# A gated convolution and MLP mixer on one core: weight loads on another queue, some row sums on another engine, fused small arithmetic and a new written-out order

## The chip, the core and the metric

The kernel runs on one NeuronCore of a Trainium2 chip. Five engines work side by side, each with its own instruction list: TensorE (PE in the profile, with PEld for its weight loads), VectorE (DVE), ScalarE (ACT), GpSimd (POOL) and SyncE (SP). SyncE does no arithmetic; it issues DMA transfers. ScalarE and GpSimd can issue transfers too. The engines meet only through semaphores. The metric is the device time of one execution in microseconds (us), as the median of several runs.

## The reference, cut to what matters

The input is a sequence of S = 2048 rows with D = 640 features, all in bfloat16. Two branches are mixed by a gate for each row.

```python
x = A_q
g = sigmoid((x * gate_w).sum(-1, keepdims=True))
# branch a: shift convolution (4 taps) of k, times v, then a long convolution with ssm_k by FFT
kv = k_shift * v
y  = irfft(rfft(kv, 2S) * rfft(ssm_k, 2S))[:S] + kv * ssm_D
a  = x * y
# branch b: norm, w1, gelu, shift of four feature groups by +-1 and +-2 rows, w2; norm, w3, gelu, w4
h  = gelu(layernorm(x) @ w1)
x1 = x + shifted(h) @ w2
b  = x1 + gelu(layernorm(x1) @ w3) @ w4
return g * a + (1 - g) * b
```

layernorm subtracts the row's mean and divides by the root of its variance plus 1e-5.

## The kernel before, in words

Rows are worked in 16 tiles of 128 (t = 0 to 15), grouped in four chunks of 512 (sc = 0 to 3). Features are worked in 5 groups of 128 (c = 0 to 4) in the convolution branch. All data lives in one SBUF tensor called `arena`, and all PSUM in one called `PSall` with 8 banks. So the profile names every operand `arena` or `PSall`, and helper functions give many operations the same line: L657 is every tensor_tensor of VectorE, L662 every plain tensor_scalar, L667 every activation, L689 nearly every matmul, L234 and L237 every DMA.

The stages are these. `x_load` brings the rows of x; `ln1` takes each tile's mean and variance, has GpSimd raise the variance to the power -1/2 (L862), normalises the tile on VectorE and transposes it (tiles 0 to 7 on TensorE at L919, the rest by DMA); `mm1` multiplies by w1 and ScalarE applies the gelu; `mm2` multiplies the shifted result by w2 and adds x; `ln2`, `mm3`, `mm4` do the second half of the MLP. Beside that, for each feature group, `h_load` and `h_fold` prepare the filter, `kv` forms the four-tap convolution times v, `h_chunk` and `x_fwd` are the Fourier transforms as matmuls, `unit` multiplies the spectra on VectorE, and `final` transforms back and mixes.

Nothing is scheduled on the fly. The program first records every operation, with a number, and then emits them in the order of a hand-supplied table of numbers, `SEQUENCE`; each engine runs its own operations in that order. `PLACES` says which PSUM bank each accumulation takes, and `ON` is a string of switches that moves single operations (a scaling, a copy, an addition) between VectorE and ScalarE, or between VectorE and a DMA. An engine that waits holds back everything behind it in its list, SyncE included: a transfer that waits for its data delays the transfers behind it.

What the steps below touch. The mean and variance of the first norm come from VectorE's bn_stats (two halves of a tile, L858) and bn_aggr (L859) for all 16 tiles, since `LNS` is 16; the branch for tiles from `LNS` on is there but empty. w1 is loaded in two halves of 400 KB each and w2 in one part of 640 KB and four of 40 KB; all seven are issued by ScalarE. A VectorE copy at L732 gathers a part of both halves of w1 into `w1x`. `hx` copies (L943) move 32-row pieces of the gelu's output to their shifted places. `mmg` is the gate's dot product on TensorE, whose four results a chunk VectorE copies out of PSUM.

```python
PET, LNS, LNA = 8, 16, 4
        P.dma("act", w1[:, :, 320 * h:320 * (h + 1)], ...
    P.dma("act", w2[:, 0:4, :], ...
```

Of the kernel before, what the change touches and what calls it, by code (L numbers as in the profile page):

```python
# [8 lines left out]
ACTF = mybir.ActivationFunctionType  # L9
# [434 lines left out]
def bass_gated_mix__ssm_conv_h3__mixer_s_mlp__prompt_kernel(  # L444
# [6 lines left out]
    P = Prog(nc)  # L451
# [27 lines left out]
    def ps(n, cls):  # L479
# [3 lines left out]
    SEQUENCE = [7, 2, 1, 0, 5, 3, 6, 46, 8, 9, 4, 10, 11, 12, 13, 14, 15, 16, 17, 18, 19, 20, 21, 22, 45, 48, 52,  # L483
# [67 lines left out]
    ON = ("0000000011111111010100000010000000000100001011110000000000000010000000001101001000010100100111110010"  # L551
          "00100100001000100000000000000000000010000000000")

    HW = S + 4
    oXF = alloc(20480)
# [606 lines left out]
```

## Time and profile before

| What | Value |
|---|---|
| Median of 3 runs | 226.66 us |
| The runs | 1255.35, 226.16, 226.66 us |
| The profiled execution's own time | 224.96 us |
| Its span in the trace | 223.2 us |
| Granted TensorE clock | 0.995 of full |
| TensorE busy | 210.7 us (94%) |
| VectorE busy | 213.0 us (95%) |
| ScalarE busy | 192.6 us (86%) |
| GpSimd busy | 53.6 us (24%) |

The span is the time from the first instruction to the last in the trace; the execution's own time holds 1.8 us around it. The run of 1255.35 us is far from the other two and the median does not depend on its size. Durations in the text come from the profiled execution. The busy time of an engine is the union of its instructions' times; neighbouring instructions overlap a little, so the mean duration of one is more than the time by which it moves its engine on.

### The profile page before, as it was taken

What the parts mean: (1) busy time and instruction counts of PE and PEld (TensorE: products, weight loads), DVE (VectorE), ACT (ScalarE), POOL (GpSimd) and SP (SyncE); (2) the same over time, 40 slices, a digit from 0 to 9 for tenths busy, and PEclk for the clock granted to TensorE, in tenths of its full rate; (3) what the DMA queues carried; (4) which work ended last, traced back from release to release, by engine and by line L of the source; (5) the groups of instructions that cost most, each with busy time, mean ns of one, the idle gap of its engine ahead of it and who ended that gap; (6) DMA issues with size and microseconds to landing.
All of it is one profiled execution on the core that took longest, in us unless ns stands there. A gap on an engine that the chain in (4) does not pass through costs nothing.

```text
span 223.2 us, 3880 instructions
## 1 busy us (share of the span) xinstructions
PE 210.7 (94%) x1418; PEld 126.8 (57%) x1418; DVE 213.0 (95%) x434; ACT 192.6 (86%) x304; POOL 53.6 (24%) x57
## 2 busy tenths in 40 slices
PE   5599999999999999999999999999999999999960
PEld 2297875544566444675445665445666545777640
DVE  5999999998999998999999999999997999999994
ACT  2278999999989999998999999999999797466891
POOL 1221201240000320000132102106216662475340
PEclk9999999999999999999999999999999999999997
DMA  5996799997799994999556879699399999988788
GB/s 148 348 255 218 107 243 230 179 267 161 152 232 332 295 310 97 204 187 202 110 109 118 175 151 226 116 188 200 72 187 172 261 164 245 175 102 96 82 118 167
DMA packets 80803, 41.30 MB, mean 185 GB/s; under 512 B 59210, under 2 KB 77327, under 8 KB 80783
## 3 DMA queue, kind: packets, MB, share of 16 engines
q1 hardware_dynamic: 72080, 30.42, 59.0%
q0 software_dynamic: 6496, 8.92, 26.8%
q10 hardware_dynamic: 2206, 1.71, 2.7%
q8 instruction: 11, 0.18, 0.4%
q14 instruction: 10, 0.07, 0.1%
HBM read 14.88 MB, written 5.77 MB: 93 GB/s over the span
## 4 chain that ended last, share of the span: by engine, by line
DVE 69%; DMA 11%; ACT 8%; PE 7%; issue 2%; ACTq 1%; POOLq 0%
DVE arena L657 59%; ACT arena L667 8%; DMA arena<-arena 7%; PE PSall L689 7%; DMA arena<-in_B_w_dram 4%; DVE arena L662 4%; DVE arena L858 3%; DVE arena L943 2%; DVE arena L978 1%; ACTq L237 1%; DVE arena L859 1%; ACT L715 0%; DVE arena L732 0%; ACT arena L715 0%; POOLq L389 0%
## 5 line engine op out<-in xcount | busy, mean ns | idle before, releaser
L689 PE MATMUL PSall<-arena 128*128 128x512 bf16 (+5 forms) x1357 | 203.0, 309 | 3.6 <-DVE arena L657 1.9
L657 DVE TENSOR_TENSOR arena<-arena 128x1024 bf16<-128x1024 bf16 (+14 forms) x279 | 174.7, 688 | 2.6 <-DMA arena<-arena 1.0
L689 PEld LDWEIGHTS PSall<-arena 128*128 128x128 bf16 x1357 | 122.6, 98 | 83.1 <-ACT arena L667 3.2
L667 ACT ACTIVATE arena<-PSall 128x512 bf16<-128x512 f32 (+8 forms) x157 | 96.4, 673 | 14.8 <-PE PSall L919 8.5
L667 ACT ACTIVATE arena<-arena 128x640 bf16<-128x640 bf16 (+5 forms) x89 | 82.9, 959 | 3.5 <-DVE arena L657 3.4
L862 POOL TENSOR_TENSOR arena<-arena 128x2 f32<-128x2 f32 (+2 forms) x15 | 17.4, 1161 | 70.2 <-DVE arena L662 36.2
L237 POOL DMA_DIRECT2D arena<-arena x14 | 12.4, 886 | 77.6 <-DVE arena L657 71.5
L237 POOL DMA_DIRECT2D out_dram<-arena x24 | 24.6, 1299 | 16.1 <-ACT arena L667 8.3
L667 ACT ACTIVATE arena<-PSall,arena 128x640 bf16<-128x640 f32 (+2 forms) x32 | 20.3, 657 | 6.9 <-PE PSall L689 6.8
L858 DVE BATCH_NORM_STATS2 arena<-arena 128x6 f32<-128x320 bf16 x32 | 14.4, 480 | 1.7 <-DMA arena<-in_A_q_dram 1.6
L662 DVE TENSOR_SCALAR arena<-arena 128x640 bf16<-128x640 bf16 (+8 forms) x51 | 13.8, 289 | 0.1
L978 DVE SCALAR_TENSOR_TENSOR arena<-PSall,arena 128x640 bf16<-128x640 f32 x12 | 9.7, 814 | 0.5 <-PE PSall L689 0.5
L712 PE MATMUL PSall<-arena 128*128 128x512 bf16 x15 | 5.3, 521 | 2.3 <-DVE arena L709 2.3
L919 PE MATMUL PSall<-arena 128*128 128x128 bf16 x40 | 3.5, 219 | 2.0 <-DVE arena L662 2.0
L712 PEld LDWEIGHTS PSall<-arena 128*128 128x128 bf16 x15 | 1.8, 129 | 5.0 <-issue 2.4
L943 DVE TENSOR_SCALAR arena<-arena 32x256 bf16<-32x256 bf16 (+1 forms) x18 | 4.1, 229 | 0.3
L919 PEld LDWEIGHTS PSall<-arena 128*128 128x128 bf16 x40 | 2.4, 97 | 2.9 <-DVE arena L662 2.2
L859 DVE BATCH_NORM_AGGREGATE arena<-arena 128x2 f32<-128x12 f32 x16 | 2.8, 193 | 0.1
L667 ACT ACTIVATE PSall<-PSall 128x640 f32<-128x640 f32 x4 | 2.8, 698 | 0.1
L667 ACT ACTIVATION_READ_ACCUMULATOR arena<-arena 128x1 f32 x12 | 2.4, 198 | 0.0
L715 ACT ACT_TABLE_LOAD x1 | 1.3, 1283 | 1.2 <-PEq L1147 1.2
L662 DVE TENSOR_SCALAR arena<-PSall 128x4 f32<-128x4 f32 x4 | 0.6, 156 | 0.3 <-PE PSall L689 0.3
(22 smaller groups left out, 5.5 us busy)
## 6 DMA issues: line engine op xcount, KB each, us to landing
arena<-arena POOLq DMA_DIRECT2D x8, 512.0 KB, 5.8
arena<-in_A_ssm_k_dram SPq DMA_DIRECT2D x5, 512.0 KB, 4.5
arena<-in_A_q_dram SPq DMA_DIRECT2D x6, 320.0 KB, 6.1
arena<-in_B_w_dram SPq DMA_DIRECT2D x1, 1920.0 KB, 10.1
out_dram<-arena SPq DMA_DIRECT2D x16, 96.0 KB, 3.4
arena<-arena POOLq DMA_DIRECT2D x6, 256.0 KB, 3.4
out_dram<-arena POOLq DMA_DIRECT2D x16, 96.0 KB, 5.0
arena<-in_A_q_dram SPq DMA_DIRECT2D x8, 192.0 KB, 4.7
```

The costliest lines, as they stand in the source:

```text
L237: fn = lambda e: e.dma_start(out, in_, **kw)
L657: P.op(eng, lambda e: e.tensor_tensor(o, real(a), real(b), op), [a, b], [o], dve_ns(o, [a, b], 2) if eng == "dve" else 500)
L662: P.op(eng, lambda e: e.tensor_scalar(o, real(a), s1, s2, op0=op0, **({} if op1 is None else {"op1": op1})), [a] + aps, [o], dve_ns(o, [a] ...
L667: P.op("act", lambda e: e.activation(real(o), real(a), f, bias=bias, scale=scale, **({"accum_out": accum} if accum is not None else {})), ...
L689: fns.append(lambda e, l=l, r=r, i=i: e.matmul(real(o), l, r, start=(i == 0), stop=(i == last)))
L712: P.op("pe", lambda e: e.matmul(real(pw), warm[:, 0:128], warm[:, 128:640], start=True, stop=True), [warm], [pw], 427.0 if i < 14 else 216.0)
L858: P.op("dve", lambda e, o=o, i=i: e.bn_stats(o, i), [i], [o], 400)
L859: P.op("dve", lambda e: e.bn_aggr(bna[:, t, :], bns[k]), [bns[k]], [bna[:, t, :]], 120)
L862: P.op("pool", lambda g: g.tensor_tensor(o, a, e, ALU.pow), [a, e], [o], dur)
L919: P.op("pe", [lambda e, c=c, pb=pb, xn=xn: e.transpose(real(pb)[:, 128 * c:128 * (c + 1)], xn[:, 128 * c:128 * (c + 1)], ident) for c in r ...
L943: P.op("dve", lambda e, o=hT[q, 4, c0:c0 + n], i=hx[q, :]: e.tensor_scalar(o, i, 1.0, None, op0=ALU.mult), [hx[q, :]], [hT[q, 4, c0:c0 + n ...
L978: P.op("dve", lambda e: e.scalar_tensor_tensor(x, real(pr), 1.0, x, op0=ALU.mult, op1=ALU.add, accum_out=st[1, 0][:, t:t + 1]), [pr, x], [ ...
```

## The change

Six things change together.

1. The loads of w1 and w2 are issued by SyncE instead of ScalarE.
2. `LNS` goes from 16 to 12: for tiles 12 to 15 the row sum and the sum of squares of the first norm come from two ScalarE passes with an accumulated output, in place of bn_stats and bn_aggr on VectorE.
3. The small arithmetic on the norms' statistics and on the gate uses scalar_tensor_tensor, which does two operations in one instruction; the second norm's normalisation becomes x * rstd + off on VectorE too.
4. ScalarE instead of VectorE copies the gate's dot products out of PSUM.
5. `ON` sets other switches. Counted in the built programs: two of the 128x2048 tap scalings, one copy of 1x1024, one normalisation and three 128x256 scalings go from ScalarE to VectorE, three copies of 1x512 go the other way; four more `hx` copies of 32x512 are on VectorE instead of SyncE; three more additions of 128x1024 are on VectorE and one of 128x2048 fewer (the others are accumulating DMAs of GpSimd).
6. `SEQUENCE` and `PLACES` are new throughout.

The core of the diff; of the two tables only the first line is shown.

```diff
-    SEQUENCE = [7, 2, 1, 0, 5, 3, 6, 46, 8, 9, 4, 10, 11, 12, 13, 14, 15, 16, 17, 18, 19, 20, 21, 22, 45, 48, 52,
...
+    SEQUENCE = [2, 1, 5, 4, 0, 26, 3, 8, 9, 10, 11, 12, 13, 14, 15, 16, 25, 45, 50, 49, 17, 18, 48, 28, 68, 51, 27,
...
-    st = {(l, f): small(NT) for l, f in [(0, 3), (0, 5)] + [(1, f) for f in range(6)]}
+    st = {(l, f): small(NT) for l, f in [(0, 3), (0, 5)] + [(1, f) for f in (0, 1, 3, 4, 5)]}
...
-    st.update({(0, 0): bna[:, :, 1], (0, 1): gst[3], (0, 4): gst[5]})
+    st.update({(0, 1): gst[3], (0, 4): gst[5]})
...
-        P.dma("act", w1[:, :, 320 * h:320 * (h + 1)], B_w1[:, 320 * h:320 * (h + 1)].rearrange("(c p) f -> p c f", p=128),
+        P.dma(sp, w1[:, :, 320 * h:320 * (h + 1)], B_w1[:, 320 * h:320 * (h + 1)].rearrange("(c p) f -> p c f", p=128),
               bias=(9.5e8, 8.9e8)[h], early=True).lat += 400.0
...
-    P.dma("act", w2[:, 0:4, :], bass.AP(B_w2.tensor, B_w2.offset, [[D, 128], [160 * D, 4], [1, D]]), bias=5e8, early=True)
+    P.dma(sp, w2[:, 0:4, :], bass.AP(B_w2.tensor, B_w2.offset, [[D, 128], [160 * D, 4], [1, D]]), bias=5e8, early=True)
     for g in range(4):
-        P.dma("act", w2[32 * g:32 * (g + 1), 4, :], B_w2[160 * g + 128:160 * g + 160, :], bias=4e8, early=True)
+        P.dma(sp, w2[32 * g:32 * (g + 1), 4, :], B_w2[160 * g + 128:160 * g + 160, :], bias=4e8, early=True)
...
+    def stt(o, a, x, b, op0, op1):
+        aps = [x] if not isinstance(x, float) else []
+        P.op("dve", lambda e: e.scalar_tensor_tensor(o, a, x, b, op0=op0, op1=op1), [a, b] + aps, [o], n_of(o) / 0.96 + 65)
...
             if a >= LNS:
-                var_of(0, a, b)
-                ts(bna[:, a:b, 0], st[0, 0][:, a:b], 1.0 / D, None, ALU.mult)
+                tt(st[0, 4][:, a:b], mean, mean, ALU.mult)
+                stt(st[0, 3][:, a:b], st[0, 1][:, a:b], 1e-5, st[0, 4][:, a:b], ALU.add, ALU.subtract)
...
-    def var_of(l, a, b):
-        s = {f: st[l, f][:, a:b] for f in (0, 1, 3, 4)}
-        tt(s[4], s[0], s[0], ALU.mult)
-        ts(s[4], s[4], 1.0 / D ** 2, 1e-5, ALU.mult, ALU.subtract)
-        tt(s[3], s[1], s[4], ALU.subtract)
-
     def ln_math(l, a, b):
-        var_of(l, a, b)
-        pool_pow(st[l, 5][:, a:b], st[l, 3][:, a:b], neghalf[:, a:b])
-        ts(st[l, 2][:, a:b], st[l, 0][:, a:b], -1.0 / D, None, ALU.mult)
-        tt(st[l, 4][:, a:b], st[l, 2][:, a:b], st[l, 5][:, a:b], ALU.mult)
+        s = {f: st[l, f][:, a:b] for f in (0, 1, 3, 4, 5)}
+        stt(s[4], s[0], 1.0 / D ** 2, s[0], ALU.mult, ALU.mult)
+        stt(s[3], s[1], 1e-5, s[4], ALU.add, ALU.subtract)
+        pool_pow(s[5], s[3], neghalf[:, a:b])
+        stt(s[4], s[0], -1.0 / D, s[5], ALU.mult, ALU.mult)
...
-    PET, LNS, LNA = 8, 16, 4
+    PET, LNS, LNA = 8, 12, 4
...
-            act(xn1[t // 2 % 2][:, t % 2], X[:, t, :], ACTF.Copy, accum=st[0, 0][:, t:t + 1])
+            act(xn1[t // 2 % 2][:, t % 2], X[:, t, :], ACTF.Copy, scale=1.0 / D, accum=bna[:, t, 0:1])
...
-        ts(gst[0][:, 4 * sc:4 * sc + 4], pg, 1.0, None, ALU.mult)
+        scale(gst[0][:, 4 * sc:4 * sc + 4], pg, 1.0, False)
...
-        ts(gst[2], bna[:, :, 0], gsum[:, 0:1], None, ALU.mult)
-        tt(gst[1], gst[1], gst[2], ALU.add)
+        stt(gst[1], bna[:, :, 0], gsum[:, 0:1], gst[1], ALU.mult, ALU.add)
...
-                ts(xn, x, mean, rstd, ALU.add, ALU.mult)
+                ts(xn, x, rstd, off, ALU.mult, ALU.add)
```

SyncE's list from its start, before the change: `in_A_q_dram` is x, `in_A_ssm_k_dram` the filter, `in_A_k_dram` is k.

```order
L237 DMA arena<-in_A_q_dram 128x640 x3
L237 DMA arena<-in_A_q_dram 128x2x640
L237 DMA arena<-in_A_q_dram 128x640
L237 DMA arena<-in_A_q_dram 128x2x640 x3
L237 DMA arena<-in_A_ssm_k_dram 128x2048
L234 DMA_TRANSPOSE arena<-in_A_k_dram 128x2048
L237 DMA arena<-in_A_q_dram 128x2x640 x2
L234 DMA_TRANSPOSE arena<-arena 128x16x128
```

The same list after the change, from its second row on (four single tiles of x stand ahead of it); 128x5x320 is a half of w1, 32x640 and 128x4x640 are parts of w2, and the transpose of 128x16x128 is that of the folded filter of group 0.

```order
L237 DMA arena<-in_A_q_dram 128x2x640
L237 DMA arena<-in_B_w_dram 128x5x320 x2
L237 DMA arena<-in_A_q_dram 128x2x640
L237 DMA arena<-in_B_w_dram 32x640
L237 DMA arena<-in_A_ssm_k_dram 128x2048
L237 DMA arena<-in_A_q_dram 128x2x640
L237 DMA arena<-in_B_w_dram 32x640 x2
L237 DMA arena<-in_A_q_dram 128x2x640
L234 DMA_TRANSPOSE arena<-in_A_k_dram 128x2048
L237 DMA arena<-in_B_w_dram 32x640
L234 DMA_TRANSPOSE arena<-arena 128x16x128
L237 DMA arena<-in_B_w_dram 128x4x640
```

w1 now stands behind the first six tiles of x, and the large part of w2 stands behind the transposes of k and of the folded filter.

VectorE's list just ahead of the copy into `w1x`, before the change: the copy is the row at L732.

```order
L858 BN_STATS arena<-arena 128x6 x2
L859 BN_AGGR arena<-arena 128x2 x3
L662 TENSOR_SCALAR arena<-arena 128x1
L662 TENSOR_SCALAR arena<-arena 128x640
L858 BN_STATS arena<-arena 128x6 x3
L732 TENSOR_SCALAR arena<-arena 128x640
L662 TENSOR_SCALAR arena<-arena 128x2
L858 BN_STATS arena<-arena 128x6
```

The same place after the change, where the copy is the row at L731.

```order
L857 BN_STATS arena<-arena 128x6
L661 TENSOR_SCALAR arena<-arena 128x1
L857 BN_STATS arena<-arena 128x6 x2
L858 BN_AGGR arena<-arena 128x2
L731 TENSOR_SCALAR arena<-arena 128x640
L858 BN_AGGR arena<-arena 128x2
L661 TENSOR_SCALAR arena<-arena 128x640
L661 TENSOR_SCALAR arena<-arena 128x2
```

The copy has moved forward: 12 bn_stats of VectorE stand ahead of it now, and 15 stood there before.

ScalarE's list after the change, at the place where `mm2` of the tiles 0 to 3 is taken from PSUM: a plain 128x640 from `arena` to `arena` is a pass of the first norm's sums of tiles 12 to 15.

```order
L666 ACTIVATE arena<-PSall 128x4
L666 ACTIVATE arena<-arena 128x640
L666 ACTIVATE PSall,arena<-PSall 128x2x320
L666 ACTIVATE arena<-arena 128x640 x2
L666 ACTIVATE arena<-PSall 128x640 x2
L666 ACTIVATE PSall,arena<-PSall 128x2x320
L666 ACTIVATE arena<-arena 128x640 x2
L666 ACTIVATE PSall,arena<-PSall 128x2x320
L666 ACTIVATE arena<-arena 128x640 x2
```

Seven of the eight new passes stand between these evictions of PSUM; the eighth follows a little later.

More of the change, by code (lines that the diff above doesn't have):

```diff
@@ L481, in ps @@
         return v if n == 1 else v.rearrange("p (b n) -> p b n", b=2)
-    SEQUENCE = [7, 2, 1, 0, 5, 3, 6, 46, 8, 9, 4, 10, 11, 12, 13, 14, 15, 16, 17, 18, 19, 20, 21, 22, 45, 48, 52,
[60 rows of a table removed]
-    PLACES = [5, 3, 4, 3, 7, 2, 6, 4, 0, 5, 3, 5, 1, 0, 7, 5, 2, 2, 0, 6, 5, 2, 7, 0, 1, 0, 4, 3, 2, 6, 5, 2, 1, 0,
[6 rows of a table removed]
-    ON = ("0000000011111111010100000010000000000100001011110000000000000010000000001101001000010100100111110010"
-          "00100100001000100000000000000000000010000000000")
+    SEQUENCE = [2, 1, 5, 4, 0, 26, 3, 8, 9, 10, 11, 12, 13, 14, 15, 16, 25, 45, 50, 49, 17, 18, 48, 28, 68, 51, 27,
[59 rows of a table added]
+    PLACES = [7, 0, 4, 2, 5, 7, 5, 7, 4, 2, 0, 5, 4, 0, 1, 6, 6, 2, 5, 4, 1, 7, 4, 1, 4, 1, 3, 6, 2, 2, 1, 1, 0, 6,
[6 rows of a table added]
+    ON = ("0000000011111111111111110101110110010100010000101111000000100000011000000000110000000001010010001001"
+          "001000100100001000000000000000000000000000101001001")
     HW = S + 4
@@ L865, in bn_math @@
         for a, b in ((t0, t1),) if t0 >= 4 else ((t, t + 1) for t in range(t0, t1)):
+            mean, var = bna[:, a:b, 0], bna[:, a:b, 1]
             if a >= LNS:
-                var_of(0, a, b)
-                ts(bna[:, a:b, 0], st[0, 0][:, a:b], 1.0 / D, None, ALU.mult)
+                tt(st[0, 4][:, a:b], mean, mean, ALU.mult)
+                stt(st[0, 3][:, a:b], st[0, 1][:, a:b], 1e-5, st[0, 4][:, a:b], ALU.add, ALU.subtract)
             else:
-                ts(st[0, 3][:, a:b], bna[:, a:b, 1], 1e-5, None, ALU.add)
+                ts(st[0, 3][:, a:b], var, 1e-5, None, ALU.add)
             pool_pow(st[0, 5][:, a:b], st[0, 3][:, a:b], neghalf[:, a:b], 750)
-    def var_of(l, a, b):
-        s = {f: st[l, f][:, a:b] for f in (0, 1, 3, 4)}
-        tt(s[4], s[0], s[0], ALU.mult)
-        ts(s[4], s[4], 1.0 / D ** 2, 1e-5, ALU.mult, ALU.subtract)
-        tt(s[3], s[1], s[4], ALU.subtract)
-    def ln_math(l, a, b):
-        var_of(l, a, b)
-        pool_pow(st[l, 5][:, a:b], st[l, 3][:, a:b], neghalf[:, a:b])
-        ts(st[l, 2][:, a:b], st[l, 0][:, a:b], -1.0 / D, None, ALU.mult)
-        tt(st[l, 4][:, a:b], st[l, 2][:, a:b], st[l, 5][:, a:b], ALU.mult)
+    def ln_math(l, a, b):
+        s = {f: st[l, f][:, a:b] for f in (0, 1, 3, 4, 5)}
[3 more added lines that the diff above has]
+        stt(s[4], s[0], -1.0 / D, s[5], ALU.mult, ALU.mult)
     def ln_turn(l, t, xn):
@@ L984, in ln2 @@
         for t in range(t0, t1):
-            x, xn, mean, rstd = X[:, t, :], xn2[t // 2 % 2][:, t % 2], st[1, 2][:, t:t + 1], st[1, 5][:, t:t + 1]
+            x, xn, off, rstd = X[:, t, :], xn2[t // 2 % 2][:, t % 2], st[1, 4][:, t:t + 1], st[1, 5][:, t:t + 1]
             if turn(t >= LNA):
-                act(xn, x, ACTF.Identity, scale=rstd, bias=st[1, 4][:, t:t + 1])
+                act(xn, x, ACTF.Identity, scale=rstd, bias=off)
             else:
-                ts(xn, x, mean, rstd, ALU.add, ALU.mult)
+                ts(xn, x, rstd, off, ALU.mult, ALU.add)
             ln_turn(1, t, xn2[t // 2 % 2])
```

131 rows, old and new, of tables (PLACES, SEQUENCE) are left out of this document.

## The prediction

> **What bounds the kernel now.** I read the page first: busy times, the 40 slices, and the shares of the chain that ended last.
>
> ```profile
> PE 210.7 (94%) x1418; PEld 126.8 (57%) x1418; DVE 213.0 (95%) x434; ACT 192.6 (86%) x304; POOL 53.6 (24%) x57
> ...
> PE   5599999999999999999999999999999999999960
> ...
> DVE  5999999998999998999999999999997999999994
> ACT  2278999999989999998999999999999797466891
> ...
> DVE 69%; DMA 11%; ACT 8%; PE 7%; issue 2%; ACTq 1%; POOLq 0%
> ```
>
> VectorE works for 213.0 of 223.2 us, so all its waits together are 10.2 us. TensorE is nearly as full. To see where the rest is lost I asked for the busy time of each engine by stretches (time, then busy us of PE, PEld, DVE, ACT, POOL; last the DMA share and GB/s).
>
> ```profile
> 0.00:5.00 5.00, 2.73 (x7) 1.04 (x8) 2.60 (x14) 1.49 (x2) 0.41 (x5) 1.00 0.51 125
> 5.00:10.00 5.00, 3.45 (x22) 1.43 (x19) 4.54 (x16) 0.70 (x1) 1.62 (x3) 1.00 1.09 345
> 10.00:15.00 5.00, 4.17 (x66) 3.81 (x66) 4.64 (x18) 3.42 (x11) 1.39 (x2) 1.00 1.18 306
> ...
> 25.00:30.00 5.00, 5.00 (x42) 3.84 (x40) 4.90 (x17) 5.00 (x12) 0.00 (x0) 1.00 0.90 212
> ...
> 35.00:40.00 5.00, 5.00 (x48) 2.98 (x47) 5.00 (x12) 5.00 (x7) 0.00 (x0) 1.00 1.10 215
> ...
> 100.00:110.00 10.00, 10.00 (x56) 5.33 (x55) 10.00 (x10) 9.40 (x17) 0.88 (x1) 1.00 0.82 144
> ```
>
> And, since a busy TensorE need not be one at its pace, the timeline of one full stretch of it:
>
> ```profile
> 99.83 4.45 PE L689 MATMUL PSall<-arena 128*128 128x384 bf16 x28
> ```
>
> 28 matmuls in 4.45 us are 159 ns each, back to back: here TensorE has no slack. So from 25 us on two engines are full side by side, and the granted clock is 1.00. An engine that is relieved there gives time back only if the other also gets through earlier. What is open is the start: in the first 15 us TensorE has 10.4 us busy, part of it warming up, and VectorE 11.8. The start sets how early the full stretch begins; VectorE's work sets how long it lasts. The timeline of the start, with the waits in brackets, and one piece of the chain:
>
> ```profile
> 0.75 4.81 SPq L237 DMA_DIRECT2D arena<-in_A_q_dram  x8
> ...
> 2.48 1.37 ACTq L237 DMA_DIRECT2D arena<-in_B_w_dram  x3
> ...
> 3.38 0.89 DVE L858 BATCH_NORM_STATS2 arena<-arena 128x6 f32<-128x320 bf16 x2 [1.17 <-DMA arena<-in_A_q_dram]
> ...
> 6.12 7.93 SPq L234 DMA_TRANSPOSE arena<-in_A_k_dram  x1
> 6.17 0.49 DVE L858 BATCH_NORM_STATS2 arena<-arena 128x6 f32<-128x320 bf16 x1 [0.43 <-DMA arena<-in_A_q_dram]
> ...
> 10.83 0.73 PE L689 MATMUL PSall<-arena 128*128 128x128 bf16 x10 [0.80 <-ACT arena L667]
> ...
> 11.02 1.27 DVE L858 BATCH_NORM_STATS2 arena<-arena 128x6 f32<-128x320 bf16 x3
> ...
> 12.65 0.33 DVE L732 TENSOR_SCALAR arena<-arena 128x640 bf16<-128x640 bf16 x1 [0.36 <-DMA arena<-in_B_w_dram]
> ```
> ```profile
> 3.31 9.32 DMA arena<-in_B_w_dram
> ```
>
> The second half of w1 was issued at 3.31 us and landed at 12.63, and VectorE waited for it. The first `mm1` matmul stands at 10.83.
>
> **The change, part by part: VectorE's work.** The groups of instructions with shapes kept apart (count, busy us, mean ns of one):
>
> ```profile
> L657 DVE TENSOR_TENSOR arena<-arena 128x2048 bf16<-128x2048 bf16 x57 | 68.3, 1217 | 1.5 <-DMA arena<-arena 1.0 <-DMA arena<-in_A_v_dram 0.3
> L657 DVE TENSOR_TENSOR arena<-arena 128x1024 bf16<-128x1024 bf16 x84 | 54.9, 680 | 0.2
> L667 ACT ACTIVATE arena<-arena 128x2048 bf16<-128x2048 bf16 x17 | 34.0, 2010 | 0.0
> L667 ACT ACTIVATE arena<-arena 128x640 bf16<-128x640 bf16 x28 | 22.9, 836 | 0.4 <-DVE arena L657 0.4
> L858 DVE BATCH_NORM_STATS2 arena<-arena 128x6 f32<-128x320 bf16 x32 | 14.4, 480 | 1.7 <-DMA arena<-in_A_q_dram 1.6
> L978 DVE SCALAR_TENSOR_TENSOR arena<-PSall,arena 128x640 bf16<-128x640 f32 x12 | 9.7, 814 | 0.5 <-PE PSall L689 0.5
> L662 DVE TENSOR_SCALAR arena<-arena 128x640 bf16<-128x640 bf16 x16 | 6.5, 429 | 0.0
> L859 DVE BATCH_NORM_AGGREGATE arena<-arena 128x2 f32<-128x12 f32 x16 | 2.8, 193 | 0.1
> L662 DVE TENSOR_SCALAR arena<-arena 128x2048 bf16<-128x2048 bf16 x3 | 2.2, 747 | 0.0
> L662 DVE TENSOR_SCALAR arena<-arena 128x2 f32<-128x2 f32 x10 | 1.6, 157 | 0.0
> L662 DVE TENSOR_SCALAR arena<-arena 1x512 bf16<-1x512 bf16 x3 | 0.8, 279 | 0.0
> L662 DVE TENSOR_SCALAR arena<-PSall 128x4 f32<-128x4 f32 x4 | 0.6, 156 | 0.3 <-PE PSall L689 0.3
> L943 DVE TENSOR_SCALAR arena<-arena 32x512 bf16<-32x512 bf16 x2 | 0.6, 304 | 0.0
> L662 DVE TENSOR_SCALAR arena<-arena 128x384 bf16<-128x384 bf16 x1 | 0.3, 316 | 0.0
> ```
>
> By busy over count. Removed: 8 bn_stats at 0.45 us (3.6), 4 aggregates at 0.18 (0.7), 27 small ones at 0.16 (4.3), 4 copies out of PSUM at 0.15 (0.6), 3 of 1x512 at 0.27 (0.8), one 128x2048 addition at 1.20: 11.2 us. Added: 18 small scalar_tensor_tensor, two 128x2048 taps at 0.73 (1.5), three 128x1024 additions at 0.65 (2.0), four 32x512 copies at 0.30 (1.2), one 128x640 at 0.41, three 128x256 at no more than the 0.30 of 128x384 (0.9), one 1x1024 at twice 0.27 (0.5).
>
> A small scalar_tensor_tensor is not in this trace. The nearest by size is the 128x2 tensor_scalar at 0.16 us; the same operation stands there only at 128x640 out of PSUM, 0.81 us. Below, 18 cost 2.9 us; above, 14.6. I take the lower end, because the size is a few elements, and keep the other as a rare case. Added then: 9.4 us; net 1.8 us less.
>
> These busy times overlap: three bn_stats in a row took 1.27 us, 0.42 each against the mean of 0.48, so 0.06 of each lies beside its neighbour. The change takes 47 instructions and puts 32, 15 fewer; 15 times 0.05 is 0.75 us that the rows count and the engine does not gain. **VectorE's work: 1.1 us less.** The Trainium skill, "Perfetto Trace Analysis", section "Optimizing Scalar/DVE Operations", says that profiled latency is about twice the engine-busy time of the overhead of about 60 ns on SBUF. The trace agrees in direction: by that figure the nine fewer small instructions alone would be worth 0.5 us where the 157 ns of their row give 1.4.
>
> **The start.** SyncE issues eight loads of x in 4.81 us; ScalarE issues three of w1 and w2 in 1.37 us, 0.46 each, which I take for the first few. After four single tiles and one pair the two halves of w1 go out at about 0.75 + 5 x 0.46 = 3.1 and 3.5 us, as late as before. Sizes, from the DMA issues by line:
>
> ```profile
> arena<-in_B_w_dram ACTq DMA_DIRECT2D x2, 400.0 KB, 7.9
> arena<-in_A_q_dram SPq DMA_DIRECT2D x4, 160.0 KB, 3.5
> ```
>
> Up to the end of w1 that queue holds six tiles of 160 KB and two halves of 400 KB, 1.80 MB. By the stretches above the DMA engines moved 0.63 MB by 5 us and 345 GB/s after: 1.80 MB by 8.4 us, an estimate. The next pairs of x come behind w1 instead of beside it. VectorE reaches the copy into `w1x` after 12 bn_stats (12 x 0.42), 5 aggregates and 4 small ones (about 0.1 each) and two normalisations (0.4 each), 6.7 us behind its first at 3.38: at 10.1 us. So w1 is there, and the wait of 0.36 goes. The wait of 0.43 for a single tile goes too, if x no longer shares the engines with w1. **0.8 us less waiting on VectorE.** The wait of 1.17 for the first tile stays. TensorE gains as well: the second tile is normalised one bn_stats pair and more earlier, so the first `mm1` comes at about 9.1 instead of 10.83.
>
> By the Trainium skill, "DMA: Bandwidth & Descriptors", section "Issuing engines are not separate DMA queues", all queues run on the same 16 DMA engines and interleave, so a change of queue saves only issue time; this speaks against the 0.8, and it is the second rival below.
>
> **ScalarE.** Eight passes of 128x640 at 0.82 us come in (6.6), and two taps at 2.0 (4.0) and one normalisation go; with the small moves it is some 1.5 us more, most of it between 25 and 50 us, where the rows show it full: 5.00 of 5. What hides it: its seven DMA issues go, and the last of them stood in its list at 16.9 us:
>
> ```profile
> 16.93 0.71 ACTq L237 DMA_DIRECT2D arena<-in_B_w_dram  x1
> ```
>
> The first three of the seven (1.37 us) lay ahead of its first work, so they hid nothing. The four others, 0.33 each for three and 0.71, were 1.7 us among the evictions. I cost ScalarE at nothing. If that cover is gone, TensorE waits up to 1.5 us for PSUM.
>
> **The sum.** VectorE has 1.1 us less to do and waits 0.8 less; TensorE begins 1.7 earlier, so it does not hold VectorE back. 224.96 - 1.9 = 223.1 us against the profiled execution. That execution is 1.7 us under the median of 226.66, so on that scale I say **224.8 us**. The new order in the middle, the banks and the order of the `final` steps I cost at nothing: VectorE's other waits come to 10.2 - 1.17 - 0.43 - 0.36 = 8.2 us, the empty ends of the span among them, so there is little to win there and as much to lose.
>
> **The rivals.** *First, slower: the large part of w2 comes late.* ScalarE issued it at 16.93 us. Now it stands on SyncE behind the transpose of k and that of the folded filter.
>
> ```profile
> 22.93 3.13 SPq L234 DMA_TRANSPOSE arena<-arena  x1
> ```
> ```profile
> 27.55 0.73 ACT L667 ACTIVATE arena<-PSall 128x640 bf16<-128x640 f32 x1
> ```
>
> The transpose of k held SyncE until 14.05, and the folded filter's issue takes 3.13 us once VectorE is through with it, at about 16. So w2 goes out at 19 to 20. The first eviction of `mm2` stood at 27.55; TensorE, 1.7 earlier and with the matmuls of that tile still to do, would want w2 at about 24. If w2 needs the 9.3 us of w1 it lands at 29; TensorE stands 5 us, ScalarE and VectorE behind it, and the time is 224.8 + 5 = 230. It turns the sign from 2 us, a landing after 26. For it: nothing passes a waiting SyncE. Against: by then DMA is at 212 GB/s, not 345. 0.14.
>
> *Second: w1 lands no sooner than before*, at 12.6, since what is moved ahead of it is the same. VectorE then waits 12.6 - 10.1 = 2.5 us at `w1x` instead of 0.36, and time is 226.66 - 1.1 - 0.4 + 2.1 = 227.3. For it: the DMA share stands at 1.09 and 1.18, full. Against: of these bytes some were x pairs and the filter that now come behind. 0.14.
>
> *Third: TensorE bounds, and the change does not do what it says.* VectorE's 1.1 us become waiting, and the start is no earlier, because TensorE's first work is still set by the evictions of the transposed tiles (the 0.80 in the row at 10.83): 226.7. For it: TensorE is full from 25 us on and has the same matmuls. Against: its first wait ends with a tile that VectorE now gives sooner. 0.2.
>
> *Fourth: the start gives more*, because TensorE and ScalarE both had holes there (4.17 and 3.42 of 5 at 10 to 15), and two engines that are fed earlier take another 2.6 of VectorE's 8.2 us of other waits away, beside the 0.8: 226.66 - 1.1 - 3.4 = 222.2. For it: `w1x` and the first `mm1` move by two us. Against: in the full stretch there is nothing to catch up with. 0.15.
>
> *Rare:* the small fused operation costs like the large: 18 x 0.65 = 11.7 us more, 236. 0.02.
>
> **How the numbers follow.** The forecast itself has 0.35. Two per cent, 4.5 us, is about what a measurement of this kernel can tell from no change. Faster by that, under 222.1, needs the fourth rival and a little more: 0.11. Slower, over 231.2, needs the first with w2 still later than 30, or the rare case: 0.09. The range runs from 221.8 to 229.8: it takes in most of the fourth and nearly all of the first, and leaves out 0.2.
>
> **What would show it.** Right: the first `mm1` matmul at 9 to 9.5 us; no wait over 0.2 at the `w1x` copy; VectorE busy about 212 us, its small fused rows near 0.16; the first `mm2` eviction at 26 or before. Wrong: a wait of TensorE for a DMA of `in_B_w_dram` near 25 us (first rival); a wait of 2 us at `w1x` (second); VectorE idle for TensorE, several us more than before, with the end unmoved (third); ScalarE full and TensorE waiting for it between 25 and 60 us, which would break my cover.

## The result: 229.64 us, 1.3 per cent slower

The changed kernel takes 229.64 us (median; 229.21 to 229.93) against 226.93 for the kernel before on the same chip. The ratio is 1.013 with a 95% interval of 1.0095 to 1.0164. That is less than the two per cent that the forecast called no change and inside its range, but on the wrong side. It is close to the 230 us of the first rival, which the range was drawn to take in; that rival's mechanism did not occur, so the nearness is luck.

The page of the changed kernel, to be read against that of the kernel before. Line numbers are one lower than before for most helpers (L656 is the tensor_tensor of VectorE, L666 the activation); the small scalar_tensor_tensor is L862 and the power on GpSimd L865.

```profile
span 227.8 us, 3867 instructions
...
PE 211.9 (93%) x1418; PEld 125.7 (55%) x1418; DVE 213.0 (93%) x419; ACT 192.9 (85%) x320; POOL 64.5 (28%) x55
...
DVE  5999999999999879999899999999998899989994
...
DVE 34%; PE 33%; DMA 23%; issue 5%; SPq 2%; ACT 1%; POOL 1%; POOLq 0%
```

VectorE is busy for 213.0 us in both kernels. Its idle time, span less busy, went from 223.2 - 213.0 = 10.2 to 227.8 - 213.0 = 14.8 us: these 4.6 us are the loss. In the chain that ended last, DMA rose from 11 to 23 per cent. GpSimd's busy time rose by 11 us, although it has two instructions fewer. The groups by line and shape say what VectorE waits for:

```profile
L656 DVE TENSOR_TENSOR arena<-arena 128x2048 bf16<-128x2048 bf16 x56 | 66.9, 1217 | 4.0 <-DMA arena<-arena 3.7
L656 DVE TENSOR_TENSOR arena<-arena 128x1024 bf16<-128x1024 bf16 x87 | 56.5, 684 | 1.9 <-DMA arena<-arena 1.6
...
L661 DVE TENSOR_SCALAR arena<-arena 128x2048 bf16<-128x2048 bf16 x5 | 3.7, 740 | 0.0
...
L862 DVE SCALAR_TENSOR_TENSOR arena<-arena 128x4 f32<-128x4 f32 x9 | 1.4, 153 | 1.1 <-POOL arena L865 0.9
L862 DVE SCALAR_TENSOR_TENSOR arena<-arena 128x2 f32<-128x2 f32 x8 | 1.2, 149 | 0.0
```

Waiting for a transfer from `arena` to `arena` stood at 1.0 us before and is 3.7 + 1.6 = 5.3 now; 0.9 us for the power on GpSimd is new. With some 0.5 us saved at the start this gives 5.3 - 1.0 + 0.9 - 0.5 = 4.7, the loss. These transfers are the additions that GpSimd issues as accumulating DMAs. They are read from two profiles; the experiments below test them. The timeline of VectorE, around 79, 113 and 175 us:

```profile
78.38 0.69 DVE L656 TENSOR_TENSOR arena<-arena 128x1016 bf16<-128x1016 bf16 x1
81.23 1.22 DVE L656 TENSOR_TENSOR arena<-arena 128x2048 bf16<-128x2048 bf16 x1 [2.17 <-DMA arena<-arena]
...
101.13 0.15 DVE L862 SCALAR_TENSOR_TENSOR arena<-arena 128x4 f32<-128x4 f32 x1
101.21 11.50 DVE L656 TENSOR_TENSOR arena<-arena 128x2048 bf16<-128x2048 bf16 x11
113.63 0.16 DVE L862 SCALAR_TENSOR_TENSOR arena<-arena 128x4 f32<-128x4 f32 x1 [0.92 <-POOL arena L865]
...
172.07 5.56 DVE L656 TENSOR_TENSOR arena<-arena 128x2048 bf16<-128x2048 bf16 x9 [0.83 <-DMA arena<-arena]
178.54 10.10 DVE L656 TENSOR_TENSOR arena<-arena 128x1024 bf16<-128x1024 bf16 x15 [0.91 <-DMA arena<-arena]
```

And that of GpSimd:

```profile
72.72 1.07 POOL L237 DMA_DIRECT2D arena<-arena  x1 [2.61 <-DMA arena<-arena]
...
101.37 12.23 POOL L865 TENSOR_TENSOR arena<-arena 128x4 f32<-128x4 f32 x1 [25.26 <-DVE arena L862]
113.57 1.77 POOL L237 DMA_DIRECT2D arena<-arena  x2
```

Three places are to be seen. GpSimd issues an accumulating DMA at 72.72 us, having waited 2.61 us for an earlier transfer, and VectorE waits 2.17 us for it at 79 us. At 101.37 us GpSimd begins the power of `ln2-8-12` on 128x4 elements and needs 12.23 us, while VectorE runs eleven tensor_tensors in a row without a gap (nine of 128x2048 or 128x2047 and two of 128x1024; a row of the timeline names the first shape only); then VectorE waits for that power, and two accumulating DMAs queue behind it on GpSimd, of which one makes VectorE wait 0.46 us more at 120.55. After 170 us accumulating DMAs are late again. None of this was in the forecast.

The start went as forecast. SyncE's rows, then TensorE's:

```profile
3.15 1.04 SPq L237 DMA_DIRECT2D arena<-in_B_w_dram  x2
```
```profile
8.93 0.84 PE L688 MATMUL PSall<-arena 128*128 128x128 bf16 x15
10.03 1.65 PE L688 MATMUL PSall<-arena 128*128 128x128 bf16 x25 [0.26 <-DMA arena<-in_B_w_dram]
```

### The profile page after: what moved, and what is told of

It is laid out like the page before. It is cut to its first block, busy times and chain, and to the rows that moved or that the text cites. A ratio compares the mean times of both kernels' runs of the same rounds, so it can differ in the third digit from the quotient of the medians.

```text
span 227.8 us, 3867 instructions
## 1 busy us (share of the span) xinstructions
PE 211.9 (93%) x1418; PEld 125.7 (55%) x1418; DVE 213.0 (93%) x419; ACT 192.9 (85%) x320; POOL 64.5 (28%) x55
## 4 chain that ended last, share of the span: by engine, by line
DVE 34%; PE 33%; DMA 23%; issue 5%; SPq 2%; ACT 1%; POOL 1%; POOLq 0%
PE PSall L688 33%; DVE arena L656 29%; DMA arena<-arena 18%; DMA arena<-in_B_w_dram 3%; DVE arena L661 2%; DMA arena<-in_A_v_dram 2%; DVE arena L942 1%; ACT arena L666 1%; SPq L237 1%; DVE arena L976 1%; PE PSall L918 1%; DVE arena L857 0%; SPq L234 0%; POOL out_dram L237 0%; POOL arena L237 0%
## 5 line engine op out<-in xcount | busy, mean ns | idle before, releaser
L688 PE MATMUL PSall<-arena 128*128 128x256 bf16 (+5 forms) x1357 | 204.7, 309 | 8.0 <-ACT arena L666 3.8
L656 DVE TENSOR_TENSOR arena<-arena 128x1024 bf16<-128x1024 bf16 (+10 forms) x267 | 175.2, 715 | 6.4 <-DMA arena<-arena 5.3
L666 ACT ACTIVATE arena<-PSall 128x512 bf16<-128x512 f32 (+8 forms) x161 | 96.6, 655 | 13.0 <-PE PSall L688 7.8
L666 ACT ACTIVATE arena<-arena 128x640 bf16<-128x640 bf16 (+6 forms) x93 | 83.6, 923 | 11.6 <-DVE arena L656 11.2
L865 POOL TENSOR_TENSOR arena<-arena 128x2 f32<-128x2 f32 (+2 forms) x15 | 29.8, 1984 | 88.7 <-DVE arena L862 70.8
L237 POOL DMA_DIRECT2D out_dram<-arena x24 | 26.1, 1346 | 21.5 <-DVE arena L656 9.7
L666 ACT ACTIVATE arena<-PSall,arena 128x640 bf16<-128x640 f32 (+2 forms) x32 | 20.6, 652 | 3.5 <-PE PSall L688 3.2
L857 DVE BATCH_NORM_STATS2 arena<-arena 128x6 f32<-128x320 bf16 x24 | 10.7, 479 | 1.7 <-DMA arena<-in_A_q_dram 1.5
L942 DVE TENSOR_SCALAR arena<-arena 32x256 bf16<-32x256 bf16 (+1 forms) x22 | 5.2, 238 | 0.4
L666 ACT ACTIVATION_READ_ACCUMULATOR arena<-arena 128x1 f32 x20 | 4.4, 218 | 0.0
L862 DVE SCALAR_TENSOR_TENSOR arena<-arena 128x4 f32<-128x4 f32 (+2 forms) x18 | 2.8, 155 | 1.1 <-POOL arena L865 0.9
L666 ACT ACTIVATE PSall<-PSall 128x640 f32<-128x640 f32 x4 | 3.1, 766 | 0.0
```

Of the source, the lines that this page charges most:

```text
L237: fn = lambda e: e.dma_start(out, in_, **kw)
L656: P.op(eng, lambda e: e.tensor_tensor(o, real(a), real(b), op), [a, b], [o], dve_ns(o, [a, b], 2) if eng == "dve" else 500)
L666: P.op("act", lambda e: e.activation(real(o), real(a), f, bias=bias, scale=scale, **({"accum_out": accum} if accum is not None else {})), ...
L688: fns.append(lambda e, l=l, r=r, i=i: e.matmul(real(o), l, r, start=(i == 0), stop=(i == last)))
L857: P.op("dve", lambda e, o=o, i=i: e.bn_stats(o, i), [i], [o], 400)
L862: P.op("dve", lambda e: e.scalar_tensor_tensor(o, a, x, b, op0=op0, op1=op1), [a, b] + aps, [o], n_of(o) / 0.96 + 65)
```

## The experiments

Theory A: the new order costs the time, and the parts are neutral or a gain. Theory B: a part costs the time (SyncE's queue, or the work given to ScalarE). By parts I mean (1) w1 and w2 on SyncE, (2) the first-norm sums of four tiles on ScalarE, (3) the fused arithmetic, (4) the gate sums copied by ScalarE. "Order" means the table of the order together with the PSUM banks and the switches that put single operations on VectorE, ScalarE or a DMA. Lines in rows of the experiments are four higher than in the changed kernel (L660 is its L656, L670 its L666, L866 its L862, L869 its L865).

### Parts and order apart

```diff
 kernel before, own order (e1)
-P.dma("act", w1 ...)  P.dma("act", w2 ...)
+P.dma(sp, w1 ...)     P.dma(sp, w2 ...)
-small norm and gate arithmetic, unfused
+the same in scalar_tensor_tensor
-ts(gst[0] ..., pg ...)       # VectorE
+scale(gst[0] ..., pg, ...)   # ScalarE
```

> The kernel before with its own order, places and PSUM banks, and the change's parts alone: w1 and w2 on SyncE, the small norm and gate arithmetic fused, the gate sums copied by ScalarE; the first-norm sums of tiles 12 to 15 stay with bn_stats. Theory A (the new order costs the time, the parts are neutral or a gain): 224.5 to 226.5 us, first mm1 matmul near 9 to 10 us, no wait of VectorE over 1 us for an accumulating DMA. Theory B (the parts cost the time): 228 us or more.

Measured: 223.48 us, ratio 0.988 (0.982 to 0.993).

```diff
 kernel before, own order (e4)
-P.dma("act", w1 ...)  P.dma("act", w2 ...)
+P.dma(sp, w1 ...)     P.dma(sp, w2 ...)
```

> The kernel before with w1 and w2 alone put on SyncE's queue. Theory A: 225 to 226.9 us (the start as in the changed kernel, 0.8 to 1.7 us sooner, of which the full middle may take a part back). Theory B, if SyncE's queue is the part that costs: 228 to 229 us. If w2's large part comes late (my first rival): a wait of TensorE for it near 25 us.

Measured: 223.72 us, ratio 0.989 (0.985 to 0.994). The move of w1 and w2 to SyncE alone makes the kernel 1.1 per cent faster; fusing and the ScalarE copy add nothing that can be measured, though VectorE's busy time falls from 212.8 to 212.0 us. Both are faster than both kernels and lie below the range of Theory A too. Theory B falls for parts 1, 3 and 4 in the old order. Why the gain ends there may be seen in the chain of the fourth experiment, whose first share was VectorE's before:

```profile
PE 81%; DVE 11%; DMA 5%; ACT 1%; issue 1%
```

TensorE has most of the chain now, and 52 per cent of it in the first experiment. That TensorE sets the end there is read from these two chains and was not tried.

```diff
 changed kernel, own order (e2)
-parts 1, 2, 3, 4
+as in the kernel before, each operation where its successor stands
```

> The changed kernel with its new order, places and banks, and all four parts undone: w1 and w2 on ScalarE's queue, bn_stats for tiles 12 to 15, the unfused arithmetic, the gate sums copied by VectorE. Theory A: 229.5 to 232 us, as slow as the changed kernel or slower by what the start gave (up to 2 us), with VectorE again waiting 2 us for the first accumulating DMA near 80 us. Theory B: 226 to 227.5 us.

```diff
 changed kernel, own order (e3)
-P.dma(sp, w1 ...)     P.dma(sp, w2 ...)
+P.dma("act", w1 ...)  P.dma("act", w2 ...)
```

> The changed kernel with w1 and w2 alone put back on ScalarE's queue. Theory A: 229.6 to 231.5 us, the first mm1 matmul back near 10.8 us and the waits from 79 us on unchanged. Theory B, if SyncE's queue is the part that costs: 227 to 228 us.

Measured: 247.29 us (1.093) and 243.15 us (1.076), far over both theories. The edits carried a fault of their own: at their old numbers the loads of w1 and w2 now stood in ScalarE's list behind its first evictions. In the third, VectorE waits 6.2 us at `w1x` and TensorE twice nearly 6 us for w1 and w2. The second was not mended, so the new order without any of the parts has no clean run. For the third I put the issues back to where the kernel before has them:

```diff
 ScalarE's list (e9, on e3)
-small loads, evictions, w1, eviction, w1, evictions, w2 ...
+small loads, w2 (40 KB), w1, w1, evictions, w2 ...
```

> The changed kernel with w1 and w2 on ScalarE's queue, and their issues put where the kernel before has them in ScalarE's list: three ahead of its first work, the other four between its first evictions (in the third experiment they stood behind ScalarE's first work). Theory A (the new order costs the time, the queue of w1 is worth 1 to 2.5 us): 230.3 to 232.3 us. If ScalarE's queue in itself were what made the third experiment slow: 240 us or more.

Measured: 233.27 us, ratio 1.032 (1.023 to 1.042). That is 1.9 per cent over the changed kernel, some 4.3 us, more than the 1 to 2.5 that I expected. ScalarE's queue and VectorE's wait, from the timelines:

```profile
2.45 1.37 ACTq L237 DMA_DIRECT2D arena<-in_B_w_dram  x3
```
```profile
14.37 0.33 DVE L735 TENSOR_SCALAR arena<-arena 128x640 bf16<-128x640 bf16 x1 [3.75 <-DMA arena<-in_B_w_dram]
```

ScalarE issues w1 even sooner (the halves at 2.80 and 3.27 us, against 3.15 and 3.66 on SyncE), but they land at 10.07 and 14.35 instead of 8.79 and 9.90. The difference that I see is that on SyncE the later rows of x stand behind w1, while beside ScalarE's queue they are issued at 3.15 and 4.18 us and travel with it; that was not tried by itself. The Trainium skill, "DMA: Bandwidth & Descriptors", section "Issuing engines are not separate DMA queues", says that transfers started by different engines run on the same DMA engines and interleave, so that a further queue saves only issue time. The landings agree: issued 0.35 us sooner on ScalarE, the first half of w1 lands 1.28 us later. That the gain comes from the place in the line is what remains, and is argued.

### The sums on ScalarE, in either order

```diff
 changed kernel, own order (e12)
-PET, LNS, LNA = 8, 12, 4
+PET, LNS, LNA = 8, 16, 4
```

> The changed kernel with the first-norm sums of tiles 12 to 15 back on VectorE (8 bn_stats and 4 aggregates, 4.3 us, in the place of the ScalarE passes) and the two small operations that the ScalarE path needs gone. If the ScalarE sums are a gain because VectorE bounds the time: 231 to 233.5 us. If TensorE or the late DMAs set the end, or ScalarE's 6.6 us cost as much as they save: 228.8 to 230.3 us.

Measured: 233.29 us, ratio 1.032 (1.024 to 1.040); VectorE is busy for 216.2 us, 3.2 more. In the new order the sums on ScalarE are worth at least what they take off VectorE.

```diff
 kernel before, own order, with parts 1, 3, 4 (e13, on e1)
-PET, LNS, LNA = 8, 16, 4
+PET, LNS, LNA = 8, 12, 4      # scratch of these passes: xn2
```

> The kernel before in its own order with all four parts, the sums of tiles 12 to 15 on ScalarE at the places where bn_stats stood (their unused outputs go to the buffers of the second norm, which are free then). If the ScalarE sums take 3 to 4 us off VectorE and ScalarE hides them, as the twelfth experiment says of the new order: 220 to 221.5 us. If ScalarE, full between 25 and 50 us in this order, hands its 6.6 us on to TensorE: 223 to 227 us, no better than the first experiment (223.48).

Measured: 229.24 us, ratio 1.014 (1.007 to 1.022): 2.6 per cent worse than without the sums and outside both expectations, though VectorE has 3.1 us less to do. The page's busy times of the first experiment, then of this one, and this one's waits of VectorE from its timeline:

```profile
PE 209.8 (94%) x1410; PEld 126.6 (57%) x1418; DVE 212.0 (95%) x419; ACT 193.1 (87%) x308; POOL 53.6 (24%) x57
```
```profile
PE 211.9 (94%) x1418; PEld 126.5 (56%) x1418; DVE 208.9 (92%) x409; ACT 198.2 (87%) x324; POOL 52.3 (23%) x57
```
```profile
32.84 0.22 DVE L946 TENSOR_SCALAR arena<-arena 32x256 bf16<-32x256 bf16 x1 [2.84 <-ACT arena L670]
...
47.05 0.16 DVE L866 SCALAR_TENSOR_TENSOR arena<-arena 128x2 f32<-128x2 f32 x1 [3.38 <-ACT arena L670]
```

And the busy times of the stretch from 20 to 50 us (PE, PEld, DVE, ACT, POOL), for the first experiment, this one, and the changed kernel:

```profile
sum 30.00, PE 29.84 PEld 19.30 DVE 29.63 ACT 29.91 POOL 5.84; mean PE 9.95 PEld 6.43 DVE 9.88 ACT 9.97 POOL 1.95
```
```profile
sum 30.00, PE 25.70 PEld 16.04 DVE 21.33 ACT 29.94 POOL 3.61; mean PE 8.57 PEld 5.35 DVE 7.11 ACT 9.98 POOL 1.20
```
```profile
sum 30.00, PE 28.32 PEld 17.04 DVE 29.36 ACT 28.71 POOL 9.81; mean PE 9.44 PEld 5.68 DVE 9.79 ACT 9.57 POOL 3.27
```

ScalarE is full in that stretch. In the old order the sums stand in front of its evictions; VectorE does 8.3 us less there, of which only 3.1 is work that is gone, and TensorE 4.1 us less. (Other places for the sums in the old order were not tried.) TensorE's waits for ScalarE between 25 and 60 us (sum, times, longest), in this experiment and in the changed kernel:

```profile
PE PSall L692 <- ACT arena L670: 4.0, 4, 1.9
```
```profile
PE PSall L688 <- ACT arena L666: 0.8, 1, 0.8
```

In the changed kernel ScalarE has room for the sums (28.71 of 30). What made the room is argued: the switches took operations off ScalarE, by the changed kernel's groups two of the 128x2048 taps above all (VectorE has five, not three); no run moved the switches alone. VectorE got these, and more 128x1024 additions and copies that were DMAs before: 213.0 us of work against the 208.9 of this experiment, 4.1 us given back.

Theory A has to be narrowed by this pair. With all the parts the old order (1.014) is as slow as the new one (1.013); without the sums it is the faster (0.988). So the sums cost 2.6 per cent in the old order, the new order makes them bearable, and sums and new order together are 2.5 per cent slower than neither.

### What the new order pays later

The additions of `unit-0` first:

```diff
 unit-0, its first addition (e5, on the changed kernel)
-accumulating DMA, issued by GpSimd (switch "1")
+tensor_tensor 128x2048 on VectorE  (switch "0")
```

> The changed kernel with one addition moved: the first accumulating DMA of unit-0 (issued at 72.72 us, landed at 81.21, VectorE waited 2.17 us for it) becomes a 128x2048 addition on VectorE (1.2 us). Theory A, if that late landing costs what its wait shows: 2.17 - 1.2 = 1.0 us less, 228.6 us. If the wait is slack that another wait takes over: 229.3 to 230.5 us. Theory B says nothing of it: 229.6 us.

Measured: 227.39 us, ratio 1.003 (1.001 to 1.006), some 1 per cent or 2.2 us under the changed kernel. The gain is larger than I expected from 2.17 us less 1.2: in the sixth, seventh, tenth and fourteenth experiments the wait there was 2.56 to 3.16 us, since VectorE came there sooner and the transfer landed at the same time (81.2 to 81.9 us).

```diff
 GpSimd's list (e6, on the changed kernel)
-pow ln2-8-12, add-DMA unit-1, add-DMA unit-1
+add-DMA unit-1, add-DMA unit-1, pow ln2-8-12
 VectorE's and ScalarE's lists
-the power's users where they were
+the power's users behind the small operation of 123.43 us
```

> The changed kernel with the power of ln2-8-12 on GpSimd moved behind the two accumulating DMAs of unit-1 that stood behind it in GpSimd's list, and its three users on VectorE and ScalarE moved behind the small operation at 123.4 us. Theory A, if GpSimd is held off its operands by VectorE's back-to-back 128x2048 additions: the power again takes several us or waits for the next hole, but the DMAs go out at 109 to 112 us instead of 113.6 and 114.2, the waits of 0.92 and 0.46 us on VectorE go, and the time falls by 0.5 to 1.4 us to 228.2 to 229.1. If the 12.23 us are only how the profile draws a waiting instruction: no change, 229.6.

Measured: 233.05 us, ratio 1.029, slower; my edit was at fault. The power ran in 2.36 us and the two DMAs landed early, but its users now blocked ScalarE's list:

```profile
122.08 1.43 ACT L670 ACTIVATE arena<-arena 128x640 bf16<-128x640 bf16 x2 [3.37 <-DVE arena L866]
```

VectorE in turn waited 5.04 us for ScalarE at 126.14, and what should have been a gain came out 1.6 per cent over the changed kernel. Mended:

```diff
 ScalarE's list (e10, on e6)
-the power's users before its evictions of 118 to 120 us
+the power's users behind them, at 123.7 us
```

> The sixth experiment with its own fault mended: the power of ln2-8-12 stands behind the two accumulating DMAs of unit-1, its two users on VectorE behind the small operation at 123.4 us, and its two users on ScalarE not before 123.7 us in ScalarE's list, so that ScalarE is not held up (in the sixth experiment it stood from 117.70 to 122.08). Theory A: the waits of 0.92 and 0.46 us go, 0.9 to 1.6 us less than the changed kernel, 228.0 to 228.7 us. If the waits are slack: 229.3 to 230.

Measured: 228.21 us, ratio 1.009 (1.005 to 1.014). It falls where expected, 0.8 us under the changed kernel by the ratios, though the intervals of the two overlap.

```diff
 VectorE's list (e14, on the changed kernel)
 stt ln2-8-12, add, add,
+stt ln2-14-16 (128x2),
 add, add, add, add, ... (nine more of 128x2048 and 128x1024)
```

> The changed kernel with one small VectorE operation (the first scalar_tensor_tensor of ln2-14-16, 0.15 us, at 118.84 us) put into the row of 128x2048 additions, after the second that follows the start of the power of ln2-8-12. If the power on GpSimd waits until VectorE does something other than these additions: the power ends about 0.9 us behind the small operation, near 104.5 instead of 113.6 us, VectorE's waits of 0.92 and 0.46 go, and the time is that of the tenth experiment, 228.2 us (0.8 to 1.4 us under the changed kernel). If only an empty VectorE lets it through: the power still takes 12 us, 229.6 us.

Measured: 228.13 us, ratio 1.007 (1.003 to 1.011), by the ratios some 1.4 us under the changed kernel; the intervals just overlap. VectorE's timeline, then GpSimd's:

```profile
101.92 2.36 DVE L660 TENSOR_TENSOR arena<-arena 128x2048 bf16<-128x2048 bf16 x2
104.19 0.17 DVE L866 SCALAR_TENSOR_TENSOR arena<-arena 128x2 f32<-128x2 f32 x1
104.28 9.23 DVE L660 TENSOR_TENSOR arena<-arena 128x2048 bf16<-128x2048 bf16 x9
113.42 0.15 DVE L866 SCALAR_TENSOR_TENSOR arena<-arena 128x4 f32<-128x4 f32 x1
```
```profile
102.09 3.08 POOL L869 TENSOR_TENSOR arena<-arena 128x4 f32<-128x4 f32 x1 [25.65 <-DVE arena L866]
109.26 0.89 POOL L237 DMA_DIRECT2D arena<-arena  x1 [4.08 <-DVE arena L660]
```

With 0.17 us of other work put into the row of additions, the power ends at 105.17 instead of 113.60, 0.8 us after the end of that operation, and the DMA goes out at 109.26 instead of 113.57. VectorE's wait at 113 us is gone. It was held up, then, by what VectorE ran beside it, and the small operation let it through. Both times it ended 0.89 us after the end of an addition: here 105.17 after 101.92 + 2.36 = 104.28, in the changed kernel 113.60 after 101.21 + 11.50 = 112.71.

But an unbroken row is not enough to hold a power. VectorE's and GpSimd's rows in the tenth experiment, then in the kernel before:

```profile
103.47 14.36 DVE L660 TENSOR_TENSOR arena<-arena 128x2048 bf16<-128x2048 bf16 x16
...
111.83 2.36 POOL L869 TENSOR_TENSOR arena<-arena 128x4 f32<-128x4 f32 x1
```
```profile
119.19 3.93 DVE L657 TENSOR_TENSOR arena<-arena 128x1024 bf16<-128x1024 bf16 x7
...
120.75 1.46 POOL L862 TENSOR_TENSOR arena<-arena 128x4 f32<-128x4 f32 x1 [4.53 <-DVE arena L657]
```

In both the power is done in 1.5 to 2.4 us while VectorE runs tensor_tensors on both sides of it without a break. Which of VectorE's instructions let GpSimd in is not shown.

```diff
 GpSimd's list (e7, on the changed kernel)
-six output DMAs of mm4, additions of unit-2 as DMAs
+additions of unit-2 as DMAs, six output DMAs of mm4
```

> The changed kernel with six accumulating output DMAs of mm4 (96 KB each, issued at 170.2 to 173.2 us) moved behind the accumulating additions of unit-2. Theory A, if the crowd of transfers at 163 to 184 us makes the additions and the transpose of ln2-14-16 late: the waits at 171.25 and 177.64 (0.83 and 0.91 us) and TensorE's 1.64 us at 174.38 shrink by half or more and the time falls by 1 to 2 us, 227.6 to 228.6. If they are late for another reason: within 0.4 us of 229.6.

Measured: 228.83 us, ratio 1.012 (1.006 to 1.018). The waits at 171 and 178 us fell from 0.83 and 0.91 to 0.41 and 0.63, and the time by nothing that can be told.

```diff
 changed kernel (e8)
+e5, e6 and e7 together
```

> The last three edits together: the addition on VectorE, the power later, the six output DMAs later. Theory A, if the three jams are what the new order costs: their gains add to 2.5 to 4 us, 225.6 to 227.1, no slower than the kernel before. If each only moves the wait on: 228.5 to 230.

Measured: 231.90 us, ratio 1.025; it has the fault of the sixth and says little. With the mended place:

```diff
 changed kernel (e11)
+e5 and e10 together
```

> The addition of unit-0 on VectorE (fifth experiment, 227.39 us) and the mended place of the power together. Theory A: 1 to 1.6 us less than the fifth, 225.8 to 226.5 us, level with the kernel before. If the two waits hide one another: 227 to 227.6.

Measured: 226.30 us, ratio 1.001 (0.997 to 1.006): two edits bring the changed kernel level with the kernel before.

```diff
 changed kernel (e15)
+e5, e10 and e7 together
```

> The eleventh experiment (226.30 us) with the six output DMAs of mm4 moved behind the accumulating additions of unit-2, as in the seventh. If the crowd of transfers after 163 us costs what is left against the kernel before: 224.5 to 225.5 us. If not: 226 to 226.8 us.

Measured: 226.35 us, ratio 1.000 (0.996 to 1.004). The output DMAs are not the rest. The page of the eleventh experiment points to what may be:

```profile
span 224.2 us, 3860 instructions
...
PE 211.6 (94%) x1411; PEld 126.4 (56%) x1418; DVE 213.6 (95%) x420; ACT 192.3 (86%) x320; POOL 53.5 (24%) x54
```

VectorE's idle time is 224.2 - 213.6 = 10.6 us, that of the first experiment 222.4 - 212.0 = 10.4. They wait alike, and the longer span, 1.8 us, is 1.6 us more work of VectorE. That is read from two profiles and not tried by itself.

## Why the prediction was wrong

**The start: right.** The first `mm1` matmul came at 8.93 us (9.1 was said), w1 landed at 8.79 and 9.90 (8.4), the copy into `w1x` did not wait, and the first `mm2` eviction stood at 25.29 (26 or before). TensorE's only wait for w1 or w2 was 0.26 us. The fourth experiment gives its price in the old order: 1.1 per cent, some 2.4 us, more than the 1.9 that I had for the start and VectorE's work together. I had counted VectorE's 0.8 us and nothing for TensorE's 1.7.

**First rival, w2 late: fell.** Its large part went out at 18.30, near the 19 to 20 said, but landed at 23.03, after 4.7 us and not 9.3. **Second rival, w1 no sooner: fell** in the changed kernel, and the ninth experiment shows where it would have been right, with the issues on ScalarE.

**VectorE's work, 1.1 us less: wrong in size.** Nothing was left of it, 213.0 in both pages. The price of the small fused operation was right (153 and 149 ns against 160), so the rare case fell. But a row of 0.15 us is not 0.15 us of the engine: the one at 101.13 is followed at 101.21, the one at 104.19 at 104.28. By my rows all four parts were worth 3.6 + 0.7 + 4.3 + 0.6 - 2.9 = 6.3 us with 25 instructions fewer, 5.0 with my overlap of 0.05 us for each; the thirteenth experiment measured 213.0 - 208.9 = 4.1, so the overlap was (6.3 - 4.1) / 25 = 0.09 for each. What the switches gave back to VectorE, 4.5 us by rows and 4.0 with the overlap, is 4.1. The Trainium skill, "Perfetto Trace Analysis", section "Optimizing Scalar/DVE Operations", says that the profiled latency of a small operation's overhead is about twice the time for which the engine is busy with it. The rows agree (0.15 us, and the next begins after 0.08), and I set its sentence aside.

**ScalarE costed at nothing, with the missing DMA issues as cover: wrong cover.** They were 1.7 us; the thirteenth experiment, which has them gone too, loses 2.6 per cent, and TensorE waits 4.0 us for ScalarE there, the sign that I had named. What hid the sums in the changed kernel are, as far as its rows say, the operations that the switches moved to VectorE. I had both sides of that trade in the sum and did not see that one was the price of the other.

**The new order costed at nothing: the step that failed.** I argued that there was little to win and as much to lose, and looked only for the waits that would go. VectorE's waits for accumulating DMAs went from 1.0 to 5.3 us instead, and 0.9 for the held-up power came with them; less the 0.5 saved at the start they make up its 4.6 us of new idle time. The late DMA (2.2 us in the fifth experiment) and the power (0.8 in the tenth) are the larger part; together they carry the ratio from 1.013 to 1.001. This shows what the order costs as it stands, with the sums and switches that came with it. By the first and eleventh experiments the rest, the gain of the start that the changed kernel does not keep, is the work that VectorE got back; that is read from profiles. The late DMA and the held-up power could both be asked of the order beforehand: which additions go by DMA and what is issued before them, and what VectorE runs beside each small operation on GpSimd.

**Third and fourth rival.** TensorE may bound the time, once the start is better and the order is the old one (81 per cent of the chain in the fourth experiment). The fourth, a start that gives more (222.2), has something of the first and fourth experiments, whose 223.48 and 223.72 lie between it and my forecast; the changed kernel does not keep that gain.

## What to carry to other kernels

When work is moved to an engine that is full in some stretch, look for what was moved off it to make room, and book that as the price. When an order is rewritten, ask of each transfer and of each operation on a shared resource what now runs beside it: a row of 12 us on VectorE held GpSimd's operation of 1 us here, and everything queued behind that. The engine that issues a load also sets the load's place in line among the others: moving w1 and w2 alone was worth 1.1 per cent.

## What the runs showed of the hardware

The power on 128x4 elements takes about 1 us on GpSimd when nothing holds it (1.01 at 69.10) and took 12.23 beside eleven back-to-back tensor_tensors of VectorE, 12.22 in the fifth experiment. The Trainium skill, "SBUF — State Buffer", section "Who interferes with whom", says that a tensor_tensor with both inputs in SBUF contends with GpSimd's reads, and that the ports they share are an exclusive lock. The direction agrees; but an instruction is 1.2 us here, and GpSimd was kept out over eleven of them, until a small scalar_tensor_tensor (fourteenth experiment) or an idle VectorE came. Why that operation, which also reads twice from SBUF, lets GpSimd in was not tried and stays open; so does why the power got through between back-to-back tensor_tensors at 111.83 us in the tenth experiment (2.36 us) and at 120.75 us in the kernel before (1.46 us).
